# Centring the rows ahead of a feed-forward, and multiplying the normalisation's scale in at the last addition

## The chip, the cores and the metric

The kernel runs on one core of a Trainium2 chip. The metric is the device time of one execution in microseconds (us), median over runs. Profile times are in us from the first instruction of the profiled execution, or in ns where that is said. PE is the matrix engine, DVE the vector engine, ACT the scalar (activation) engine, POOL the GpSimd engine; SP issues DMAs.

## What is computed

A linear-attention layer (RWKV style) is followed by a Fourier mixing and a feed-forward with a residual. There are 4 batches of 768 rows, 8 heads of 48 columns, so a model width of 384; the feed-forward is 1536 wide.

```
for t in range(S):                       # attention, per batch and head
    cur = outer(u * k[t], v[t])
    y[t] = r[t] @ (state + cur)
    state = w[:, None] * state + outer(k[t], v[t])
x = y, heads side by side                # (4, 768, 384)
U  = x + real(fft(fft(x, axis=1), axis=2))
un = (U - mean(U)) / sqrt(var(U) + 1e-6) # per row
out = U + maximum(un @ w_ch1, 0) @ w_ch2
```

## The kernel before, in words

**Tiling.** The attention goes in 24 chunks of 128 rows, 6 to a batch. `attend(i)` (L307) does one: DVE scales keys and receptances into `KR` (L317), PE turns them (`tp`, L327), ACT copies the turned tile out (`KRT`, L330), PE makes the scores (`A_ps`, L341), which are masked into `MA` by DVE (L348) or by ACT and POOL (L353, L355); the state goes through PE (`u_ps`, L369 and L372) and DVE (`Sst`, L376); PE sums the outputs in `yd_ps` (L391, L396, L411), ACT takes its diagonal part out (`DE`, L401), POOL multiplies it by the values (`TT`, L402), and DVE adds both into `X` (L415). `fold` (L425) makes sums and differences of a batch's rows (`EO`, `XF`), `fourier(b)` (L451) does the two transforms as matrix products: the first into `mm` (L463), copied by ACT (L470), turned round by DVE (`TR`, L479); the second (`mp`, L498 to L502), to which DVE adds X in `UF` (L508). In what follows a *half* is 384 rows, half a batch: 3 blocks of 128 rows, 8 halves `hf` in all.

**Normalisation.** For each block DVE takes statistics (`st`, L513, and `MV`, L515: mean and variance). `normed` (L519) waits for all three blocks of the half: ACT takes the square root (L524), DVE the reciprocal `rstd` (L526) and `nm`, minus mean times `rstd` (L528), and ACT writes the normalised rows `UN` in bf16, one instruction for each block, with `rstd` as scale and `nm` as bias (L533). For batch 0 PE turns `UN` (L554) and DVE copies it out to `UNT` (L557); for the others one DMA transpose for each half, issued from SP (L545), does so.

**Feed-forward.** `mlp1(hf, ft)` (L573): three matrix products on `UNT` into a PSUM tile `hp` (L582), and ACT's clamp (Relu) into `HT` (L586); 12 of them make a half. `mlp2(hf, j)` (L589): twelve products on `HT` into a PSUM tile `mo` (L598), DVE adds `UF` into `osb` (L605), and POOL issues its DMA to the output (L608); 3 of them make a half.

**PSUM.** `hp`, `mo`, the tiles of both transforms, the turned rows of batch 0 and the fillers are all called "mm" and share three buffers.

**What sets the order.** The kernel is a list of operations, each with an engine, a planned duration, what it needs (`r`), what it makes (`w`), the tiles that it takes anew (`new`) and uses, and a number `pri`. `_Schedule.order` (L100) plays the list through and decides for each engine what comes next; the program is emitted in that order, and each engine then runs its instructions strictly in it. The rule of choice is L149:

```
start = max(at, o["ready"], t + self.LATENCY)
key = (start, o["pri"], o["n"])
if pick is None or key < pick[0]:
```

The operation that can start first is taken, and `pri` decides among those that can start at the same time, lowest first. `t` comes from `room(o)` (L121): a new tile of a ring of n buffers can be taken once every operation on the tile n places before it in that ring has been planned and has ended. `pri` is 10 times the chunk's number for the attention, 10 times 6(b+1), plus 5 to 7, for the transforms and the normalisation of batch b, from 10,000 up for the feed-forward's products, and -100 for the operations that take a product out of PSUM (L470, L508, L557, L586, L605, L608). `idle` (L612) puts up to 220 fillers, products of zeros, on PE at the lowest rank where nothing else can start (planned time below 46 us).

Of the kernel before, what the change touches and what calls it, by code (L numbers as in the profile page):

```python
# [9 lines left out]
AluOp = mybir.AluOpType  # L10
Act = mybir.ActivationFunctionType
AX = mybir.AxisListType
F32 = mybir.dt.float32
# [60 lines left out]
class _Schedule:  # L74
# [18 lines left out]
    def op(self, eng, ns, fn, r=(), w=(), new=(), use=(), after=(), dma=0, pri=0, until=None):  # L93
        o = dict(eng=eng, ns=ns, fn=fn, deps=list(r), after=list(after), w=list(w), new=list(new), dma=dma, pri=pri, until=until,
                 n=len(self.ops))
        for t in set(new) | set(use):
            t.ops.append(o)
        self.ops.append(o)
# [91 lines left out]
def kernel(  # L190
# [11 lines left out]
    nc = tc.nc  # L202
    cp = ctx.enter_context(tc.tile_pool(name="cp", bufs=1))
    inp = ctx.enter_context(tc.tile_pool(name="inp", bufs=6))
    wp = ctx.enter_context(tc.tile_pool(name="wp", bufs=3))
# [32 lines left out]
    eps_t = cp.tile([128, 1], F32, name="eps_t")  # L238
# [37 lines left out]
    op = sch.op  # L276
# [3 lines left out]
    def new(pool, shape, dtype, name, bufs):  # L280
        return sch.tile((pool, shape, dtype, name), name, bufs)
# [141 lines left out]
    bat = [dict() for _ in range(B)]  # L423
# [27 lines left out]
    def fourier(b):  # L451
        X, XF = bat[b]["X"], bat[b]["XF"]
        TT = new(bp, [128, 3, 2, 386], BF16, "TT2", 2)
        TR = new(bp, [128, 3, 2, 384], BF16, "TR", 1)
        pri = 10 * (NQ * b + NQ) + 5
# [30 lines left out]

        def second(sh, j, UF, MV):
            blk = sh * 3 + j
            mp = new(ps, [128, 2, 192], F32, "mm", 3)
            st = new(wp, [128, 6], F32, "st", 3)  # L490
            src = (TT, TR)[sh]
            lo = j * 128

            def mm():
                flat = mp().rearrange("p a m -> p (a m)")
                for ri in range(2):
                    tb = hid_t[:, 0 if ri == 0 else 1 + sh, :]
                    nc.tensor.matmul(flat, lhsT=src()[:, 1, ri, lo:lo + 128], rhs=tb[:, 192:576], start=(ri == 0),  # L498
                                     stop=False, skip_group_check=True)
                    nc.tensor.matmul(flat[:, 0:192], lhsT=src()[:, 0, ri, lo:lo + 128], rhs=tb[:, 0:192],  # L500
                                     start=False, stop=False, skip_group_check=True)
                    nc.tensor.matmul(flat[:, 192:384], lhsT=src()[:, 2, ri, lo:lo + 128], rhs=tb[:, 576:768],  # L502
                                     start=False, stop=(ri == 1), skip_group_check=True)

            deps = [("TR", b, c) for c in range(3)] if sh else [("TT2", b, c, p) for c in range(3) for p in range(2)]
            p2 = pri + 1 + sh
            op("PE", 660, mm, r=deps + ["hid"], w=[("mp", b, blk)], new=[mp], use=[src], pri=p2)
            op("DVE", 550, lambda: nc.vector.tensor_tensor(  # L508
                out=UF()[:, j, :].rearrange("p (m a) -> p a m", a=2), in0=mp(),
                in1=X()[:, blk, :].rearrange("p (m a) -> p a m", a=2), op=AluOp.add),  # L510
               r=[("mp", b, blk)], w=[("UF", b, blk)], new=[UF] if j == 0 else [], use=[mp, UF, X],
               after=[("UF", b, sh * 3)] if j else [], pri=-100)
            op("DVE", 550, lambda: nc.vector.bn_stats(out=st(), in_=UF()[:, j, :]), r=[("UF", b, blk)],  # L513
               w=[("st", b, blk)], new=[st], use=[UF], pri=p2)
            op("DVE", 170, lambda: nc.vector.bn_aggr(out=MV()[:, j, :], in_=st()), r=[("st", b, blk)],  # L515
               w=[("MV", b, blk)], new=[MV] if j == 0 else [], use=[MV, st],
               after=[("MV", b, sh * 3)] if j else [], pri=p2)

        def normed(sh, UF, UNT, MV):  # L519
            p2 = pri + 1 + sh  # L520
            rstd = new(wp, [128, 3], F32, "rstd", 3)
            nm = new(wp, [128, 3], F32, "nm", 3)
            UN = new(wp, [128, 3, DM], BF16, "UN", 2)
            op("ACT", 300, lambda: nc.scalar.activation(out=rstd(), in_=MV()[:, :, 1], func=Act.Sqrt, bias=eps_t[:, 0:1]),  # L524
               r=[("MV", b, sh * 3 + j) for j in range(3)], w=[("sd", b, sh)], new=[rstd], use=[MV], pri=p2)
            op("DVE", 170, lambda: nc.vector.reciprocal(out=rstd(), in_=rstd()), r=[("sd", b, sh)],  # L526
               w=[("rstd", b, sh)], use=[rstd], pri=p2)
            op("DVE", 150, lambda: nc.vector.scalar_tensor_tensor(  # L528
                out=nm(), in0=MV()[:, :, 0], scalar=-1.0, in1=rstd(), op0=AluOp.mult, op1=AluOp.mult),
               r=[("rstd", b, sh)], w=[("nm", b, sh)], new=[nm], use=[MV, rstd], pri=p2)  # L530

            def norm(j):
                op("ACT", 705, lambda: nc.scalar.activation(  # L533
                    out=UN()[:, j, :], in_=UF()[:, j, :], func=Act.Identity, scale=rstd()[:, j:j + 1],
                    bias=nm()[:, j:j + 1]), r=[("nm", b, sh), ("UF", b, sh * 3 + j)], w=[("UN", b, sh, j)],
                   new=[UN] if j == 0 else [], use=[UN, UF, rstd, nm], after=[("UN", b, sh, 0)] if j else [], pri=p2)

            for j in range(3):
                norm(j)
            if b == 0:  # L540
                for j in range(3):
                    turned(sh, j, UN, UNT)
                op("NONE", 0, lambda: None, r=[("UNT", b, sh, j) for j in range(3)], w=[("UNT", b, sh)])
                return
            op("SP", 1200, lambda: nc.sync.dma_start_transpose(  # L545
                out=UNT().rearrange("p j c t -> p (j c) t"), in_=UN().rearrange("p j d -> p (j d)")),
               r=[("UN", b, sh, j) for j in range(3)], w=[("UNT", b, sh)], new=[UNT], use=[UN], dma=1500, pri=-1000)
# [13 lines left out]
        for sh in range(2):  # L561
            UF = new(bp, [128, 3, DM], F32, "UF", 5)
            UNT = new(bp, [128, 3, 3, 128], BF16, "UNT", 5)
            MV = new(wp, [128, 3, 2], F32, "MV", 3)
            for j in range(3):
                second(sh, j, UF, MV)
            normed(sh, UF, UNT, MV)
            bat[b]["halves"].append((UF, UNT))


    HTs = {}

    def mlp1(hf, ft, pri):  # L573
        UF, UNT = bat[hf // 2]["halves"][hf % 2]
        if ft == 0:
            HTs[hf] = new(bp, [128, 12, 384], BF16, "HT", 3)
        HT = HTs[hf]
        hp = new(ps, [128, 384], F32, "mm", 3)

        def mm():  # L580
            for dt in range(3):
                nc.tensor.matmul(hp(), lhsT=W1[:, dt, ft * 128:(ft + 1) * 128], rhs=UNT()[:, :, dt, :],  # L582
                                 start=(dt == 0), stop=(dt == 2))

        op("PE", 495, mm, r=[("UNT", hf // 2, hf % 2), "W1"], w=[("hp", hf, ft)], new=[hp], use=[UNT], pri=pri)
        op("ACT", 490, lambda: nc.scalar.activation(out=HT()[:, ft, :], in_=hp(), func=Act.Relu), r=[("hp", hf, ft)],  # L586
           w=[("HT", hf, ft)], new=[HT] if ft == 0 else [], use=[hp, HT], after=[("HT", hf, 0)] if ft else [], pri=-100)

    def mlp2(hf, j, pri):  # L589
        b, sh = divmod(hf, 2)  # L590
        UF, UNT = bat[b]["halves"][sh]
        HT = HTs[hf]
        mo = new(ps, [128, DM], F32, "mm", 3)
        osb = new(wp, [128, DM], F32, "osb", 3)

        def mm(lo, hi):
            for ft in range(lo, hi):
                nc.tensor.matmul(mo(), lhsT=HT()[:, ft, j * 128:(j + 1) * 128], rhs=W2[:, ft, :],  # L598
                                 start=(ft == 0), stop=(ft == 11))

        op("PE", 985, lambda: mm(0, 6), r=[("HT", hf, ft) for ft in range(6)] + ["W2"], w=[("mo", hf, j, 0)], new=[mo],
           use=[HT], pri=pri)
        op("PE", 985, lambda: mm(6, 12), r=[("HT", hf, ft) for ft in range(6, 12)] + [("mo", hf, j, 0)],
           w=[("mo", hf, j)], use=[HT, mo], pri=pri)
        op("DVE", 555, lambda: nc.vector.tensor_tensor(out=osb(), in0=mo(), in1=UF()[:, j, :], op=AluOp.add),  # L605
           r=[("mo", hf, j)], w=[("osb", hf, j)], new=[osb], use=[mo, UF], pri=-100)
        row = (sh * 3 + j) * 128
        op("POOL", 550, lambda: nc.gpsimd.dma_start(out=out[b, row:row + 128, :], in_=osb()), r=[("osb", hf, j)],  # L608
           w=[("out", hf, j)], use=[osb], dma=500, pri=-100)
# [77 lines left out]
```

## Time and profile before

| what | value |
|---|---|
| three timed runs | 209.21, 210.62 and 217.61 us; median 210.62 |
| profiled execution, first to last instruction | 209.7 us |
| PE busy | 186.7 us (89%) |
| DVE busy | 136.0 us (65%) |
| ACT busy | 129.5 us (62%) |
| POOL busy | 64.0 us (31%) |
| last product starts its block of 48 | at 196.44 us |
| last addition `osb` starts | at 204.4 us |

The profiled execution has no time of its own beside the span; the span lies 0.5 us above the fastest timed run and 0.9 us below the median. Engines are counted busy for the union of their instructions; each engine's instructions are in the order of the program. A group's row gives the line, engine, operation, output and inputs, count, then busy time in us and the mean duration of one in ns, then the idle time of the engine just before them and what ended it. In the page's second part each digit is one fortieth of the span (5.24 us), in tenths; PEclk is the clock that PE was granted, in tenths of full speed.

### The profile page before, as it was taken

The page shows a single profiled execution, that of the slowest core. Times are in us where ns is not written, and L with a number is a line of the kernel's source. Part 1 is how long each engine was busy: PE and PEld are TensorE (multiplying, and loading weights), DVE is VectorE, ACT ScalarE, POOL GpSimd, SP SyncE. Part 2 cuts the span into 40 slices and gives each one's busy share as a digit, 9 for nine tenths or more (in the row PEclk, how much of TensorE's full clock was granted, in tenths as well). Part 3 has the DMA queues.
Part 4 walks back from the last instruction along what each step waited for, and adds up shares of the span by engine and source line. Part 5 has one row for each costly group of instructions (what it writes and reads, how often), then busy time and mean ns, then how long its engine had stood idle before and what let it go on. Part 6 is the DMA issues. An engine that isn't in the chain of part 4 may idle for free.

```text
span 209.7 us, 4438 instructions
## 1 busy us (share of the span) xinstructions
PE 186.7 (89%) x1729; PEld 118.7 (57%) x1731; DVE 136.0 (65%) x281; ACT 129.5 (62%) x260; POOL 64.0 (31%) x92
## 2 busy tenths in 40 slices
PE   7199975599999699999789999999999999999990
PEld 2056643267576366577457567666567665666550
DVE  5178999649999448899897999883739511111221
ACT  3467852562898686874678986987371895364300
POOL 5017793111038244442344323234110121121131
PEclk9969998569999999999969999999999999999999
DMA  5999999999759999967567000044110144112122
GB/s 103 181 188 190 258 219 210 182 191 172 125 106 164 193 179 219 219 131 150 113 144 150 12 3 0 30 104 94 41 38 0 42 99 126 38 41 75 38 75 75
DMA packets 86548, 24.73 MB, mean 118 GB/s; under 512 B 82944, under 2 KB 84608, under 8 KB 86528
## 3 DMA queue, kind: packets, MB, share of 16 engines
q1 hardware_dynamic: 82848, 17.37, 47.4%
q0 software_dynamic: 3680, 7.08, 13.3%
q8 instruction: 13, 0.21, 0.5%
q14 instruction: 7, 0.06, 0.1%
HBM read 20.32 MB, written 4.72 MB: 119 GB/s over the span
## 4 chain that ended last, share of the span: by engine, by line
PE 37%; issue 27%; DVE 11%; DMA 11%; POOL 6%; ACT 3%; SPq 2%; POOLq 0%; ACTq 0%; DVEq 0%
PE mm L598 7%; DMA vt<-in_v_dram 6%; PE mm L582 5%; DMA kr<-in_r_dram 5%; PE mm L614 4%; PE tp L327 4%; POOL out_dram L608 4%; PE mm L463 3%; DVE KR L317 3%; PE mm L498 3%; PE A_ps L341 2%; PE u_ps L369 2%; DVE XF L439 2%; DVE X L415 1%; PE yd_ps L411 1%
## 5 line engine op out<-in xcount | busy, mean ns | idle before, releaser
L586 ACT ACTIVATE HT<-mm 128x384 bf16<-128x384 f32 x96 | 45.9, 493 | 22.5 <-PE mm L582 22.1
L582 PE MATMUL mm<-UNT,W 128*128 128x384 bf16 x288 | 53.7, 330 | 0.5 <-DVE osb L605 0.3
L598 PE MATMUL mm<-W,HT 128*128 128x384 bf16 x288 | 51.1, 326 | 0.0
L605 DVE TENSOR_TENSOR osb<-mm,UF 128x384 f32<-128x384 f32 x24 | 13.3, 555 | 37.9 <-PE mm L598 37.9
L598 PEld LDWEIGHTS <-HT 128*128 128x128 bf16 x288 | 27.7, 98 | 17.6
L582 PEld LDWEIGHTS <-W 128*128 128x128 bf16 x288 | 27.3, 99 | 17.5 <-issue 1.4
L355 POOL TENSOR_SCALAR_AFFINE_SELECT MA<-AC 128x512 bf16<-128x512 bf16 x29 | 19.4, 676 | 50.4 <-ACT AC L353 49.3
L402 POOL TENSOR_TENSOR TT<-V,DE 128x384 bf16<-128x384 bf16 x24 | 25.0, 1040 | 27.7 <-ACT DE L401 27.0
L608 POOL DMA_DIRECT2D out_dram<-osb x24 | 13.3, 554 | 62.6 <-DVE osb L605 57.6
L317 DVE TENSOR_TENSOR KR<-kr,wtab 128x768 bf16<-128x768 f32 x24 | 24.9, 1044 | 8.6 <-ACT wtab L244 5.7
L330 ACT COPY KRT<-tp 128x1024 bf16<-128x1024 bf16 x24 | 24.5, 1019 | 6.2 <-PE tp L327 6.0
L353 ACT CAST AC<-A_ps 128x512 bf16<-128x512 f32 x29 | 16.6, 591 | 11.7 <-PE A_ps L341 11.7
L614 PE MATMUL mm<-zero 128*128 128x512 bf16 x71 | 20.1, 423 | 1.4 <-DVE wuc L233 1.3
L327 PE MATMUL tp<-ident,KR 128*128 128x128 bf16 x192 | 15.7, 229 | 5.8 <-DVE KR L317 5.6
L322 ACT CAST V<-vt 128x384 bf16<-128x384 f32 x24 | 12.0, 522 | 8.9 <-DMA vt<-in_v_dram 5.1
L327 PEld LDWEIGHTS <-KR 128*128 128x128 bf16 x192 | 12.4, 103 | 9.1 <-DVE KR L317 6.4
L533 ACT ACTIVATE UN<-UF,nm,rstd 128x384 bf16<-128x384 f32 x24 | 15.7, 699 | 2.8 <-DVE nm L528 2.8
L415 DVE TENSOR_TENSOR X<-yd_ps,TT 128x384 bf16<-128x384 f32 x24 | 13.1, 546 | 5.7 <-POOL TT L402 5.7
L470 ACT CAST TT<-mm 128x386 bf16<-128x386 f32 (+1 forms) x24 | 12.7, 600 | 4.3 <-PE mm L463 4.3
L331 DVE TENSOR_TENSOR PR<-KRT 128x512 bf16<-128x512 bf16 x24 | 14.1, 596 | 0.5 <-ACT KRT L330 0.4
L508 DVE TENSOR_TENSOR UF<-mm,X 128x384 f32<-128x384 f32 x24 | 12.7, 551 | 1.8 <-PE mm L502 1.1
L348 DVE TENSOR_TENSOR MA<-A_ps,mtri 128x512 bf16<-128x512 f32 x19 | 12.9, 681 | 1.1 <-PE A_ps L341 1.0
(67 smaller groups left out, 239.6 us busy)
## 6 DMA issues: line engine op xcount, KB each, us to landing
kr<-in_k_dram SPq DMA_DIRECT2D x24, 192.0 KB, 4.5
kr<-in_r_dram SPq DMA_DIRECT2D x24, 192.0 KB, 4.6
vt<-in_v_dram SPq DMA_DIRECT2D x24, 192.0 KB, 4.4
out_dram<-osb POOLq DMA_DIRECT2D x24, 192.0 KB, 2.2
W<-in_moe_w_ch_dram POOLq DMA_DIRECT2D x6, 384.0 KB, 7.7
hid_t<-hid_c SPq DMA_DIRECT2D x1, 576.0 KB, 5.1
te_t<-te_c SPq DMA_DIRECT2D x1, 289.5 KB, 4.3
to_t<-to_c SPq DMA_DIRECT2D x1, 288.0 KB, 4.0
```

The costliest lines, as they stand in the source:

```text
L317: op("DVE", 960, lambda: nc.vector.tensor_tensor(out=KR().rearrange("t s p (a d) -> t (s p) a d", a=2)[:, :, :, 0:D], in0=kr().rearrange(" ...
L327: nc.tensor.transpose(tp()[:, s, p, :], KR()[:, s, p, :], ident)
L330: op("ACT", 1010, lambda: nc.scalar.copy(KRT(), tp()), r=[("tp", i)], w=[("KRT", i)], new=[KRT], use=[tp], pri=pri)
L353: op("ACT", 590, lambda: nc.scalar.copy(AC(), A_ps[a]()), r=[("A", i)], w=[("AC", i, a)], new=[AC], use=[A_ps[a]], pri=pri)
L355: op("POOL", 680, lambda: nc.gpsimd.affine_select(out=MA[a](), in_=AC(), pattern=[[0, NP], [1, 128]], base=0, channel_multiplier=-1, compa ...
L402: op("POOL", 850, lambda: nc.gpsimd.tensor_tensor(out=TT(), in0=V(), in1=DE().unsqueeze(2).to_broadcast([128, H, D]), op=AluOp.mult), r=[( ...
L533: op("ACT", 705, lambda: nc.scalar.activation(out=UN()[:, j, :], in_=UF()[:, j, :], func=Act.Identity, scale=rstd()[:, j:j + 1], bias=nm() ...
L582: nc.tensor.matmul(hp(), lhsT=W1[:, dt, ft * 128:(ft + 1) * 128], rhs=UNT()[:, :, dt, :], start=(dt == 0), stop=(dt == 2))
L586: op("ACT", 490, lambda: nc.scalar.activation(out=HT()[:, ft, :], in_=hp(), func=Act.Relu), r=[("hp", hf, ft)], w=[("HT", hf, ft)], new=[H ...
L598: nc.tensor.matmul(mo(), lhsT=HT()[:, ft, j * 128:(j + 1) * 128], rhs=W2[:, ft, :], start=(ft == 0), stop=(ft == 11))
L608: op("POOL", 550, lambda: nc.gpsimd.dma_start(out=out[b, row:row + 128, :], in_=osb()), r=[("osb", hf, j)], w=[("out", hf, j)], use=[osb], ...
L614: op("PE", 216, lambda: nc.tensor.matmul(z(), lhsT=zero[:, 0:128], rhs=zero, start=True, stop=True), r=["zero"], w=[("idle", len(sch.ops)) ...
```

## The change

`UN` holds minus (row minus mean) instead of the normalised row: ACT computes it with the constant scale -1 and the mean as bias, and each block waits only for its own mean. The square root and the reciprocal stay, in the same places of the list but behind the centring, with `pri` 9000 in place of that of the batch (66 to 247), and no longer precede `UN`; `nm` is gone. The clamp multiplies by -1 before it clamps, which takes the sign back; since the scale of a row is positive it passes through the clamp and both products, and the last addition multiplies the row of `mo` by `rstd` (a scalar per partition) and adds `UF` in one instruction, `scalar_tensor_tensor` in place of `tensor_tensor`. It therefore waits for the reciprocal as well. The rings of `MV` and `rstd` grow from 3 to 8 buffers, and the buffer of `UF` is taken when the first product of the half is planned rather than when its addition is.

```
-            op("PE", 660, mm, r=deps + ["hid"], w=[("mp", b, blk)], new=[mp], use=[src], pri=p2)
+            op("PE", 660, mm, r=deps + ["hid"], w=[("mp", b, blk)], new=[mp, UF] if j == 0 else [mp], use=[src],
+               after=[("mp", b, sh * 3)] if j else [], pri=p2)
...
-        def normed(sh, UF, UNT, MV):
+        def normed(sh, UF, UNT, MV, rstd):
             p2 = pri + 1 + sh
-            rstd = new(wp, [128, 3], F32, "rstd", 3)
-            nm = new(wp, [128, 3], F32, "nm", 3)
             UN = new(wp, [128, 3, DM], BF16, "UN", 2)
+
+            def centre(j):
+                op("ACT", 705, lambda: nc.scalar.activation(
+                    out=UN()[:, j, :], in_=UF()[:, j, :], func=Act.Identity, scale=-1.0,
+                    bias=MV()[:, j, 0:1]), r=[("MV", b, sh * 3 + j), ("UF", b, sh * 3 + j)], w=[("UN", b, sh, j)],
+                   new=[UN] if j == 0 else [], use=[UN, UF, MV], after=[("UN", b, sh, 0)] if j else [], pri=p2)
+
+            for j in range(3):
+                centre(j)
             op("ACT", 300, lambda: nc.scalar.activation(out=rstd(), in_=MV()[:, :, 1], func=Act.Sqrt, bias=eps_t[:, 0:1]),
-               r=[("MV", b, sh * 3 + j) for j in range(3)], w=[("sd", b, sh)], new=[rstd], use=[MV], pri=p2)
+               r=[("MV", b, sh * 3 + j) for j in range(3)], w=[("sd", b, sh)], new=[rstd], use=[MV], pri=9000)
             op("DVE", 170, lambda: nc.vector.reciprocal(out=rstd(), in_=rstd()), r=[("sd", b, sh)],
-               w=[("rstd", b, sh)], use=[rstd], pri=p2)
-            op("DVE", 150, lambda: nc.vector.scalar_tensor_tensor(
-                out=nm(), in0=MV()[:, :, 0], scalar=-1.0, in1=rstd(), op0=AluOp.mult, op1=AluOp.mult),
-               r=[("rstd", b, sh)], w=[("nm", b, sh)], new=[nm], use=[MV, rstd], pri=p2)
-
-            def norm(j):
-                op("ACT", 705, lambda: nc.scalar.activation(
-                    out=UN()[:, j, :], in_=UF()[:, j, :], func=Act.Identity, scale=rstd()[:, j:j + 1],
-                    bias=nm()[:, j:j + 1]), r=[("nm", b, sh), ("UF", b, sh * 3 + j)], w=[("UN", b, sh, j)],
-                   new=[UN] if j == 0 else [], use=[UN, UF, rstd, nm], after=[("UN", b, sh, 0)] if j else [], pri=p2)
...
+               w=[("rstd", b, sh)], use=[rstd], pri=9000)
...
-            MV = new(wp, [128, 3, 2], F32, "MV", 3)
+            MV = new(wp, [128, 3, 2], F32, "MV", 8)
+            rstd = new(wp, [128, 3], F32, "rstd", 8)
...
-        op("ACT", 490, lambda: nc.scalar.activation(out=HT()[:, ft, :], in_=hp(), func=Act.Relu), r=[("hp", hf, ft)],
+        op("ACT", 490, lambda: nc.scalar.activation(out=HT()[:, ft, :], in_=hp(), func=Act.Relu, scale=-1.0), r=[("hp", hf, ft)],
...
-        op("DVE", 555, lambda: nc.vector.tensor_tensor(out=osb(), in0=mo(), in1=UF()[:, j, :], op=AluOp.add),
-           r=[("mo", hf, j)], w=[("osb", hf, j)], new=[osb], use=[mo, UF], pri=-100)
+        op("DVE", 555, lambda: nc.vector.scalar_tensor_tensor(
+            out=osb(), in0=mo(), scalar=rstd()[:, j:j + 1], in1=UF()[:, j, :], op0=AluOp.mult, op1=AluOp.add),
+           r=[("mo", hf, j), ("rstd", b, sh)], w=[("osb", hf, j)], new=[osb], use=[mo, UF, rstd], pri=-100)
```

More of the change, by code (lines that the diff above doesn't have):

```diff
@@ L510, in second @@
                 in1=X()[:, blk, :].rearrange("p (m a) -> p a m", a=2), op=AluOp.add),
-               r=[("mp", b, blk)], w=[("UF", b, blk)], new=[UF] if j == 0 else [], use=[mp, UF, X],
+               r=[("mp", b, blk)], w=[("UF", b, blk)], use=[mp, UF, X],
                after=[("UF", b, sh * 3)] if j else [], pri=-100)
@@ L517, in second @@
                after=[("MV", b, sh * 3)] if j else [], pri=p2)
-        def normed(sh, UF, UNT, MV):
+        def normed(sh, UF, UNT, MV, rstd):
             p2 = pri + 1 + sh
-            rstd = new(wp, [128, 3], F32, "rstd", 3)
-            nm = new(wp, [128, 3], F32, "nm", 3)
             UN = new(wp, [128, 3, DM], BF16, "UN", 2)
+            def centre(j):
[5 more added lines that the diff above has]
+                centre(j)
             op("ACT", 300, lambda: nc.scalar.activation(out=rstd(), in_=MV()[:, :, 1], func=Act.Sqrt, bias=eps_t[:, 0:1]),
-               r=[("MV", b, sh * 3 + j) for j in range(3)], w=[("sd", b, sh)], new=[rstd], use=[MV], pri=p2)
+               r=[("MV", b, sh * 3 + j) for j in range(3)], w=[("sd", b, sh)], new=[rstd], use=[MV], pri=9000)
             op("DVE", 170, lambda: nc.vector.reciprocal(out=rstd(), in_=rstd()), r=[("sd", b, sh)],
-               w=[("rstd", b, sh)], use=[rstd], pri=p2)
-            op("DVE", 150, lambda: nc.vector.scalar_tensor_tensor(
-                out=nm(), in0=MV()[:, :, 0], scalar=-1.0, in1=rstd(), op0=AluOp.mult, op1=AluOp.mult),
-               r=[("rstd", b, sh)], w=[("nm", b, sh)], new=[nm], use=[MV, rstd], pri=p2)
-            def norm(j):
-                op("ACT", 705, lambda: nc.scalar.activation(
-                    out=UN()[:, j, :], in_=UF()[:, j, :], func=Act.Identity, scale=rstd()[:, j:j + 1],
-                    bias=nm()[:, j:j + 1]), r=[("nm", b, sh), ("UF", b, sh * 3 + j)], w=[("UN", b, sh, j)],
-                   new=[UN] if j == 0 else [], use=[UN, UF, rstd, nm], after=[("UN", b, sh, 0)] if j else [], pri=p2)
-            for j in range(3):
-                norm(j)
+               w=[("rstd", b, sh)], use=[rstd], pri=9000)
             if b == 0:
@@ L563, in fourier @@
             UNT = new(bp, [128, 3, 3, 128], BF16, "UNT", 5)
-            MV = new(wp, [128, 3, 2], F32, "MV", 3)
+            MV = new(wp, [128, 3, 2], F32, "MV", 8)
+            rstd = new(wp, [128, 3], F32, "rstd", 8)
             for j in range(3):
                 second(sh, j, UF, MV)
-            normed(sh, UF, UNT, MV)
-            bat[b]["halves"].append((UF, UNT))
+            normed(sh, UF, UNT, MV, rstd)
+            bat[b]["halves"].append((UF, UNT, rstd))
     HTs = {}
     def mlp1(hf, ft, pri):
-        UF, UNT = bat[hf // 2]["halves"][hf % 2]
+        UF, UNT, _ = bat[hf // 2]["halves"][hf % 2]
         if ft == 0:
@@ L590, in mlp2 @@
         b, sh = divmod(hf, 2)
-        UF, UNT = bat[b]["halves"][sh]
+        UF, UNT, rstd = bat[b]["halves"][sh]
         HT = HTs[hf]
```

## The prediction

> **What bounds the kernel now.** I read the page's first two parts, then the table by stretches, the timelines of PE and DVE, the rows of the groups that change, and last the instruction order of the changed program (it can be built without running) against that of the old one.
>
> ```profile
> span 209.7 us, 4438 instructions
> PE 186.7 (89%) x1729; PEld 118.7 (57%) x1731; DVE 136.0 (65%) x281; ACT 129.5 (62%) x260; POOL 64.0 (31%) x92
> ...
> PE   7199975599999699999789999999999999999990
> ...
> DVE  5178999649999448899897999883739511111221
> ...
> PEclk9969998569999999999969999999999999999999
> ```
>
> PE bounds the kernel from about 51 us to the end, and DVE is nearly as full up to 145 us. The table by stretches (columns: stretch and length, busy us and count of PE, weight loads, DVE, ACT, POOL; granted clock; DMA share; GB/s) says how full:
>
> ```profile
> 15.50:28.30 12.80, 11.88 (x160) 7.82 (x160) 11.44 (x16) 10.14 (x20) 10.54 (x14) 1.00 1.21 229
> 35.00:40.00 5.00, 3.04 (x23) 1.92 (x24) 4.35 (x10) 1.19 (x2) 0.00 (x0) 0.52 0.97 186
> 51.36:107.00 55.64, 51.01 (x558) 33.80 (x557) 46.14 (x103) 42.02 (x85) 20.73 (x27) 1.00 0.86 159
> 107.00:111.00 4.00, 4.00 (x34) 2.46 (x34) 4.00 (x5) 2.26 (x6) 2.35 (x4) 0.59 0.63 123
> 107.00:145.70 38.70, 38.29 (x423) 25.68 (x423) 33.28 (x65) 31.30 (x66) 14.37 (x19) 0.96 0.28 59
> 145.70:196.44 50.74, 50.41 (x327) 31.01 (x324) 17.66 (x41) 28.71 (x60) 6.81 (x12) 1.00 0.19 56
> ```
>
> In 51 to 145 us PE alternates attention, transforms and feed-forward: what the attention leaves empty is filled with products of `mlp1` and `mlp2`. So the question is not what the edited instructions cost but whether the feed-forward still fills that stretch.
>
> ```profile
> 24.22 0.54 DVE L415 TENSOR_TENSOR X<-yd_ps,TT 128x384 bf16<-128x384 f32 x1
> ...
> 27.71 0.55 DVE L415 TENSOR_TENSOR X<-yd_ps,TT 128x384 bf16<-128x384 f32 x1
> ...
> 51.36 3.62 PE L614 MATMUL mm<-zero 128*128 128x512 bf16 x16
> 54.81 0.33 PE L554 MATMUL mm<-ident,UN 128*128 128x128 bf16 x3
> ...
> 196.44 7.96 PE L598 MATMUL mm<-W,HT 128*128 128x384 bf16 x48
> ```
>
> Read here: a chunk of attention without feed-forward takes 3.5 us; 16 fillers hold PE until the first normalised rows can be turned; the last 48 products end at 204.4, 5.3 us before the end.
>
> ```profile
> L586 ACT ACTIVATE HT<-mm 128x384 bf16<-128x384 f32 x96 | 45.9, 493 | 22.5 <-PE mm L582 22.1
> L533 ACT ACTIVATE UN<-UF,nm,rstd 128x384 bf16<-128x384 f32 x24 | 15.7, 699 | 2.8 <-DVE nm L528 2.8
> L605 DVE TENSOR_TENSOR osb<-mm,UF 128x384 f32<-128x384 f32 x24 | 13.3, 555 | 37.9 <-PE mm L598 37.9
> L528 DVE SCALAR_TENSOR_TENSOR nm<-MV,rstd 128x3 f32<-128x3 f32 x8 | 1.3, 162 | 0.3
> ```
>
> **What the Trainium skill says.** "Perfetto Trace Analysis", Optimization Strategy: a gap that repeats over a stretch on the engine that should be full can mean that there isn't enough PSUM for the next tile. The trace of before has no such stretch after 51 us. "SBUF — State Buffer", SBUF: two separate sides: DVE with two SBUF inputs and GpSimd exclude each other. The trace agrees in kind: `PR` (L331) takes 0.41 us beside an idle POOL and 0.86 to 1.05 in 16 to 28 us. "TensorE: Matmul & The Clock Gate", Part 1: a PE that was little used runs at half clock until it has been busy for some 3.4 us. The trace agrees: clock 0.52 in 35 to 40, and 0.59 for 4 us at 107, although PE was full there.
>
> **The small parts.** `nm` goes: 8 times 0.16 us on DVE, 1.3 in all. The centring keeps 24 ACT instructions; I take 0.70 us, as L533 (at least 0.52, as the plain copy of values L322, which has no pointers). The clamp with scale -1 stays at 0.49. `osb` with a scalar has no row of this size: `nm` (0.162) against the reciprocal's 0.170 shows no extra fixed cost, so I take 0.555, at most twice that. It lies beside PE, where a half's third of products takes 1.95 us; only the last one ends the kernel: 0 to +0.6, I take 0. The early square root is not needed for the rows of batch 0, so the planner puts 8 fillers where 16 were, and two behind: 13 against 19. PE reaches the first turning at 51.36 + 8 x 0.216 = 53.1 in place of 54.8: -1.7. No transfer is added: both programs issue the same DMAs. In the new order SP issues the two transposes of batch 1 ahead of four pairs of loads rather than two; in before they took 5.0 us to issue (102.3 to 107.3), so pair 21 lands at about 107, some 10 us before its use below.
>
> **What the change moves, the large part.** The square root and the reciprocal now have rank 9000. While DVE has attention work ready (ranks up to 240), a reciprocal that could start at the same time is put behind it. In the new order the reciprocal of half 0 stands behind the `KR` of chunk 14; that of half 1 stands behind the very last `KR`, of chunk 24. In between `X` of chunks 14 to 21 is made. But `mlp2` of half 1 has run two blocks by then, and their two tiles `mo` hold two of the three "mm" buffers until `osb`, which waits for this reciprocal. The planner's ring gives out buffers in order, so after one more `mlp1` (3 products) nothing of the feed-forward or of the transforms can be planned. PE's new order shows it: between the 36 products of `mlp2` and the transform of batch 2 stand 56 `tp`, 56 `A_ps`, 29 `u_ps`, 52 + 56 products for `yd_ps`, and those 3 products, nothing else. So DVE paces the stretch, and PE waits in it.
>
> When it begins: PE from 51.36 to there has 13 fillers (2.8 us), 18 turnings (1.0), 72 `mlp1` and 60 `mlp2` products at 0.1625 (21.5), the transforms of batch 1 (18 at 0.1635 and 36 at 0.109: 6.9) and attention for 7 to 8 chunks (62 `A_ps` at 0.041, 56 `tp` at 0.056, 64+28+32 for `yd_ps` at 0.026, 0.041 and 0.028, 24 `u_ps` 1.5 in all: 10.9), each by the distance of starts in the timeline: 43.0. Before left PE idle for 4.6 us in 51 to 107; I take 3.6: it begins at 98.0, and DVE's first wait on it, `Sst`, ends at 98.9.
>
> How long: from there to the last `KR` DVE has 7 `X`, 8 `MA`, 7 `Sst`, 9 `PR`, 8 `KR`, 2 `EO`, 2 `XF`: with the means of the page (0.546, 0.681, 0.550, 0.596, 1.044, 0.755, 0.887) 30.1 us, less 43 times the 0.09 by which neighbours overlap, 26.2. In 15.5 to 28.3 DVE was busy 89% with the same chain: 29.5. By the other way, 8 chunks at 3.5 and 3.3 for the fold, 31. PE has about 11 us of work in 31 and will be at a low clock for part of it; `tp` took 0.78 in place of 0.45 at 44.6. I add 2: 31.5, so the reciprocal comes at 130.4, and the first `osb` frees a buffer at 131.0.
>
> What is left: 35 and 72 products of the transforms (5.7, 7.9), 213 of `mlp1` (34.6), 228 of `mlp2` (37.1), attention 1.3: 86.6. Before ran such a stretch (145.7 to 196.4) without a gap. To this +2 for 4 us at half clock, as at 107, and +1 for the chain of the last fold. 131.0 + 86.6 + 3 + 5.3 = 225.9 against the span of 209.7. The median stands 0.9 above the span, the fastest run 0.5 below: 226.
>
> As a check: the stretch holds 33 us with 11 of work, so 22 us empty; given back are 1.3 (fillers), about 3 of PE's idle time after 98 us and 2 of its slow clock there: 209.7 + 22 - 6 = 226.
>
> **Rivals.** (a) *The stretch is quicker.* POOL has one mask less per chunk than in 15 to 28 us, so DVE may be held less: with the undisturbed distances (`KR` 0.87, `PR` 0.33, `MA` 0.60, `X` and `Sst` 0.465, fold 2.8) 24.0 us, clock kept: 122.9 + 0.6 + 86.6 + 5.3 = 215.4. For it: few masks on POOL. Against: POOL's 25.0 us of `TT` are unchanged, and each `X` waits for one. (b) *The chain of each chunk paces, not DVE.* At half clock PE needs 3.4 us a chunk, and each chunk hangs on one `tp` and one `yd_ps` buffer: 4.2 a chunk, 36.9 with the fold: 135.8 + 0.6 + 86.6 + 3 + 5.3 = 231, and 2 more for slow clock, 233. (c) *Not slower: DVE's pace.* The place is the same 43 operations. The end stays within 2% of before (under 214.8) if the reciprocal comes by 122, that is if they take 23 us, 0.54 each with all waits; without any wait they need 24.0, so this asks also for an earlier start: with no stall of PE after 51 us it would begin at 94.4, giving 212. (d) *The parts decide, the order doesn't:* -1.7 at 53 us and `nm` gone, 208. For it: that would be the sum if the order were kept. Against: the order is fixed in the program and shows the reciprocal behind the last `KR`.
>
> **Chances.** Forecast 0.70 (own range 220 to 231), (a) 0.13, (b) 0.12, (c) 0.03, (d) 0.02. A range from 216 to 234 leaves out about 2 in 10 and takes in the double price of the last `osb`. A difference of about 2% is what a measurement of this kernel can tell from none. Faster by more than that: 0.02; within 2%: 0.04; slower: 0.94.
>
> **What would show it.** Right: first turned rows on PE at about 53; PE's digits at 3 to 6 in slices from about 98 to 130 us, with PEclk below 9 in some; the second reciprocal at about 130, `osb` waiting for it with the products long done; from there PE full to the end, the output DMAs crowded behind it. Wrong: feed-forward products between 100 and 128 us; the second reciprocal before 120; or PE gaps after 135 us, which would say that the last stretch has a wait which I have missed.

## The result, and the profile after

The changed kernel takes 223.42 us in the median of four runs (222.4 to 224.74), the kernel before, beside it, 210.38: ratio 1.0615, 95% interval 1.0548 to 1.0681. It is 6% slower. Ratios leave out the slow executions that some kernels have now and then, such as before's of 217.61 us. The profiled execution spans 223.0 us, 13.3 more than before. Every timed run whose span is on record stands 1.7 us above it (224.74 and 223.0 here), so the profile of before, at 209.7, is an execution of about 211.4, 1 us above its median, and not one between the fastest and the median.

The page of the kernel after, the lines that answer to those shown of before (in the second part a slice is 5.58 us):

```profile
span 223.0 us, 4436 instructions
PE 193.2 (87%) x1723; PEld 123.9 (56%) x1725; DVE 139.2 (62%) x273; ACT 128.3 (58%) x260; POOL 64.8 (29%) x92
...
PE   7299965699999989997449599999999999999990
...
DVE  5268999559996998988997858956362212121131
...
PEclk9859997589999999999655569999999999999997
```

PE's share fell only from 89% to 87%, so the totals hide the loss. The second part shows its place: from the 19th slice (100 to 128 us) PE has the digits 7, 4, 4, 9, 5, where before has 7 and 8 up to 110 us and then 9 throughout. The one 9 in there stands over a PEclk of 5: PE at half speed looks full with half the work. That is also how 13.3 us more span splits: 6.8 us more idle PE (29.8 against 23.0), and 6.5 us more *busy* PE (193.2 against 186.7), although PE has six products fewer.

The table by stretches of the kernel after (columns as in the prediction):

```profile
51.36:107.00 55.64, 51.93 (x606) 35.03 (x604) 50.08 (x100) 43.71 (x91) 21.73 (x27) 1.00 0.89 163
98.00:131.00 33.00, 22.68 (x301) 17.23 (x299) 28.12 (x49) 17.39 (x32) 15.15 (x18) 0.65 0.40 77
131.00:218.00 87.00, 86.69 (x584) 53.57 (x582) 32.40 (x72) 47.23 (x101) 12.05 (x21) 0.99 0.19 56
```

Up to 98 us nothing is lost, and from 131 us PE has no gap to its last product (217.69). In between ACT, which clamps the feed-forward's products, is half idle too. What PE did with the shared buffers there, from the view of one tile's instructions ("mm", 98 to 133 us; columns: count, shortest, median and longest duration in ns, first and last start in us):

```profile
L463 PE MATMUL mm<-te_t,XF x8: 327/528/528, 128.9 to 132.8; 128*128 128x386 bf16 x8
L463 PE MATMUL mm<-to_t,XF x6: 326/474/527, 129.9 to 132.2; 128*128 128x384 bf16 x6
L595 PE MATMUL mm<-W,HT x5: 326/326/326, 97.7 to 98.4; 128*128 128x384 bf16 x5
L579 PE MATMUL mm<-UNT,W x3: 326/326/326, 100.2 to 100.5; 128*128 128x384 bf16 x3
...
L602 DVE SCALAR_TENSOR_TENSOR osb<-mm,rstd,UF x2: 609/614/619, 128.2 to 128.7; 128x384 f32<-128x384 f32 x2
```

The last products of `mlp2` (L595) end at 98.5, one `mlp1` (L579) goes at 100.2, then no product touches "mm" for 28 us. It is `osb` at 128.2 that frees a buffer, and 0.8 us later the transform (L463) begins. The timeline of DVE shows what `osb` waited for:

```profile
126.67 1.39 DVE L317 TENSOR_TENSOR KR<-kr,wtab 128x768 bf16<-128x768 f32 x1
127.98 0.16 DVE L534 RECIPROCAL rstd<-rstd 128x3 f32<-128x3 f32 x1
128.17 1.14 DVE L602 SCALAR_TENSOR_TENSOR osb<-mm,rstd,UF 128x384 f32<-128x384 f32 x2
```

A reciprocal of 0.16 us, whose root ACT had ready at 80.1 (L532, start 79.79), stands behind the last `KR`, and two tiles whose products were done by 98.5 wait for it.

### The profile page after: what moved, and what is told of

Its sections match the earlier page's. It is cut to its first block, busy times and chain, and to the rows that moved or that the text cites. A ratio compares the mean times of both kernels' runs of the same rounds, so it can differ in the third digit from the quotient of the medians.

```text
span 223.0 us, 4436 instructions
## 1 busy us (share of the span) xinstructions
PE 193.2 (87%) x1723; PEld 123.9 (56%) x1725; DVE 139.2 (62%) x273; ACT 128.3 (58%) x260; POOL 64.8 (29%) x92
## 4 chain that ended last, share of the span: by engine, by line
issue 37%; PE 28%; DVE 14%; DMA 6%; POOL 6%; ACT 5%; SPq 2%; POOLq 0%; ACTq 0%; DVEq 0%
DMA vt<-in_v_dram 6%; DVE KR L317 5%; PE mm L463 5%; PE tp L327 4%; POOL out_dram L606 4%; PE mm L595 3%; PE mm L579 3%; PE mm L612 3%; PE A_ps L341 2%; DVE EO L433 2%; ACT KRT L330 2%; PE mm L498 2%; DVE XF L439 2%; DVE MA L348 1%; DVE X L415 1%
## 5 line engine op out<-in xcount | busy, mean ns | idle before, releaser
L579 PE MATMUL mm<-UNT,W 128*128 128x384 bf16 x288 | 52.2, 326 | 0.0
L595 PE MATMUL mm<-W,HT 128*128 128x384 bf16 x288 | 49.9, 326 | 0.0
L602 DVE SCALAR_TENSOR_TENSOR osb<-mm,rstd,UF 128x384 f32<-128x384 f32 x24 | 14.7, 617 | 42.6 <-PE mm L595 42.4
L595 PEld LDWEIGHTS <-HT 128*128 128x128 bf16 x288 | 28.0, 98 | 18.4
L579 PEld LDWEIGHTS <-W 128*128 128x128 bf16 x288 | 27.5, 98 | 17.4 <-issue 0.2
L355 POOL TENSOR_SCALAR_AFFINE_SELECT MA<-AC 128x512 bf16<-128x512 bf16 x29 | 20.2, 703 | 42.8 <-ACT AC L353 34.6
L317 DVE TENSOR_TENSOR KR<-kr,wtab 128x768 bf16<-128x768 f32 x24 | 28.0, 1178 | 6.1 <-ACT wtab L244 5.8
L327 PE MATMUL tp<-ident,KR 128*128 128x128 bf16 x192 | 18.5, 254 | 10.1 <-DVE KR L317 9.5
L327 PEld LDWEIGHTS <-KR 128*128 128x128 bf16 x192 | 14.2, 114 | 13.7 <-DVE KR L317 11.2
L612 PE MATMUL mm<-zero 128*128 128x512 bf16 x65 | 19.6, 439 | 1.4 <-DVE wuc L233 1.3
L376 DVE TENSOR_TENSOR Sst<-u_ps,WD 128x384 bf16<-128x384 f32 x20 | 11.0, 550 | 6.0 <-PE u_ps L372 5.8
L463 PEld LDWEIGHTS <-XF 128*128 128x128 bf16 x72 | 7.5, 112 | 11.1 <-issue 6.4
```

Of the source, the lines that this page charges most:

```text
L317: op("DVE", 960, lambda: nc.vector.tensor_tensor(out=KR().rearrange("t s p (a d) -> t (s p) a d", a=2)[:, :, :, 0:D], in0=kr().rearrange(" ...
L327: nc.tensor.transpose(tp()[:, s, p, :], KR()[:, s, p, :], ident)
L355: op("POOL", 680, lambda: nc.gpsimd.affine_select(out=MA[a](), in_=AC(), pattern=[[0, NP], [1, 128]], base=0, channel_multiplier=-1, compa ...
L463: nc.tensor.matmul(fp(), lhsT=XF()[:, par, nb, cb * 128:(cb + 1) * 128], rhs=tab[:, nb, :], start=(nb == 0), stop=(nb == 2))
L612: op("PE", 216, lambda: nc.tensor.matmul(z(), lhsT=zero[:, 0:128], rhs=zero, start=True, stop=True), r=["zero"], w=[("idle", len(sch.ops)) ...
```

## The experiments

Edits are against the changed kernel unless said otherwise. Each ratio is to the kernel before, run beside it.

**Rank of root and reciprocal put back.** The new arithmetic stays whole.

```
-               r=[("MV", b, sh * 3 + j) for j in range(3)], w=[("sd", b, sh)], new=[rstd], use=[MV], pri=9000)
+               r=[("MV", b, sh * 3 + j) for j in range(3)], w=[("sd", b, sh)], new=[rstd], use=[MV], pri=p2)
...
-               w=[("rstd", b, sh)], use=[rstd], pri=9000)
+               w=[("rstd", b, sh)], use=[rstd], pri=p2)
```

> The changed kernel with one edit: the square root and the reciprocal get back the rank of their batch, all else stays (centring, sign, scale in the last addition). Theory (a reciprocal of rank 9000 comes late, so the last additions keep the mm buffers and PE stands empty): PE is filled between 98 and 130 us, 207 to 212 us. Rival 1 (centring earlier makes a worse order, whatever the rank): 218 or more. Rival 2 (the scaled last addition and the new waits cost by themselves): 213 to 217.

Measured: 205.92 us, ratio 0.98 (0.9703 to 0.9898), a little under what was expected; span 203.9. Its second part and its stretch:

```profile
PE   7189975689998999999999999999999999999990
```

```profile
98.00:131.00 33.00, 31.80 (x343) 21.42 (x342) 29.61 (x56) 25.34 (x53) 10.94 (x14) 1.00 0.44 92
```

The hole is gone: PE 31.80 of 33 us busy at full clock, where after had 22.68 at 0.65. All the loss comes from the rank 9000; the arithmetic itself costs nothing. The same kernel was timed again, beside one that has `pri=-100` in both places, ahead of all attention work:

> The changed kernel with root and reciprocal at the ranks of before, run again beside the one at rank -100, in more rounds: 204 to 208 us, ratio to before 0.97 to 0.985. If the gain of the first run of it (0.98) was chance, the ratio is 0.99 to 1.00.

> The changed kernel with root and reciprocal at rank -100, ahead of all attention work, in place of 9000. Theory (only the late reciprocal costs; once it is early enough, being earlier brings nothing): as with the ranks of before (203.9 us span), 204 to 208 us, ratio 0.97 to 0.99, feed-forward products throughout 98 to 131 us. Rival (the two small operations cut into DVE's chain, which is nearly full up to 145 us, and put ACT's table or a wait for the root in its way): 208 to 212, ratio 0.99 to 1.01.

Measured: 207.47 us, ratio 0.9885 (0.9813 to 0.9957) for the ranks of before; 208.8, 0.9936 (0.9902 to 0.9969) for -100. The gain of the early ranks over the kernel before is there both times, between 1 and 2%, though the second ratio lies between the two that were expected. Going first of all brings nothing more and seems to cost something: 208.8 and 0.9936 are what the rival expected, not the theory. ACT's table plays no part in it (two loads in either kernel, the last at about 10 us). Of the 3.3 us by which the profiled span is longer than its neighbour's (207.4 against 204.1), 1.2 lie ahead of the first rows turned (54.18 against 52.96), and from 51 to 98 us PE is busy 1.9 us less (44.28 against 46.19). Whether the two operations in DVE's chain do that is not shown.

**The wait taken out of `osb`, the rank left at 9000.** The scale of the rows is left out.

```
-            out=osb(), in0=mo(), scalar=rstd()[:, j:j + 1], in1=UF()[:, j, :], op0=AluOp.mult, op1=AluOp.add),
-           r=[("mo", hf, j), ("rstd", b, sh)], w=[("osb", hf, j)], new=[osb], use=[mo, UF, rstd], pri=-100)
+            out=osb(), in0=mo(), scalar=1.0, in1=UF()[:, j, :], op0=AluOp.mult, op1=AluOp.add),
+           r=[("mo", hf, j)], w=[("osb", hf, j)], new=[osb], use=[mo, UF], pri=-100)
```

> The changed kernel with rank 9000 kept, but the last addition multiplies by the constant 1.0 and does not wait for the reciprocal; the scale of the rows is left out, so the output is not the reference's. The reciprocals stay as late as in the changed kernel. Theory (the wait of the last addition on the late reciprocal is what holds the buffers): 207 to 212 us. Rival 1 (the earlier centring makes the worse order): 218 or more. Rival 3 (a late reciprocal or square root delays ACT or DVE directly): stays at 220 to 224.

Measured: 208.0 us, ratio 0.9895 (0.9814 to 0.9977). Of this kernel, DVE's timeline and the "mm" tile from 98 to 128 us:

```profile
124.56 0.16 DVE L534 RECIPROCAL rstd<-rstd 128x3 f32<-128x3 f32 x1
```

```profile
L579 PE MATMUL mm<-UNT,W x48: 323/326/327, 99.4 to 115.7; 128*128 128x384 bf16 x48
L595 PE MATMUL mm<-W,HT x24: 323/326/327, 98.5 to 121.1; 128*128 128x384 bf16 x24
```

The second reciprocal is as late as ever, but nobody needs it, and 72 feed-forward products run in the stretch where after had 8. A late reciprocal costs little by itself (span 206.0, against 203.9 with early ranks); what costs is that `osb` waits for it while it holds a buffer.

**Only half 1 late, and only half 1 early.** The rank of root and reciprocal, in the first kernel:

```
-  pri=9000
+  pri=9000 if (b, sh) == (0, 1) else p2
```

and in the second:

```
-  pri=9000
+  pri=p2 if (b, sh) == (0, 1) else 9000
```

> The changed kernel, rank 9000 for the square root and reciprocal of half 1 of batch 0 alone, the batch's rank for the other seven halves. Theory (one half's late reciprocal is enough, since it holds two of three mm buffers): the order again has a stretch of attention alone, and the time is 219 to 226 us. A rival in which all halves share the cost evenly: about an eighth of the 13 us, 210 to 213.

> The reverse: the batch's rank for half 1 of batch 0 alone, rank 9000 for the others. Its order has a shorter stretch of attention alone, later, in front of the reciprocals of the next halves (151 of PE's products against some 250). Theory: the same loss moves there and is smaller in proportion, 214 to 219 us. If half 1 were special for another reason than its buffers: 207 to 212. If the shares were even: 219 to 223.

Measured: half 1 late 222.34 us, 1.0581 (1.0473 to 1.069), as slow as the whole change: its reciprocal starts at 127.59, and between the `mlp2` product at 101 us and the transform at 128.58 PE's timeline has no product into "mm". Half 1 early 210.82 us, 1.001 (0.9953 to 1.0066): well under what was expected, and a number that the rival (half 1 is special for another reason than its buffers, 207 to 212) would have given. The trace tells them apart: the hole is there, ahead of half 2's late reciprocal (128.98), but it is shorter; the timeline of PE in the kernel with half 1 early, its products into "mm" alone:

```profile
117.91 0.65 PE L463 MATMUL mm<-to_t,XF 128*128 128x384 bf16 x3
...
129.19 1.14 PE L463 MATMUL mm<-te_t,XF 128*128 128x386 bf16 x3
```

From 118.5 to 129.2 PE has attention alone, 10.7 us, at full clock nearly to the end. The expectation took the loss from the kernel before; it has to be taken from the new arithmetic with early ranks: 210.0 - 203.9 = 6.1 us, of which 1.1 lies ahead of the first rows turned (54.19 against 53.13). That is 5.0, or 0.47 for each us of the hole. After lost 19.1, of which 1.2 lie ahead of that point: 17.9 for 128.9 - 98.5 less 0.5 of `mlp1`, 29.9 us, or 0.60 for each. The longer hole is dearer by the us, and it is the one in which the clock fell; that the rest is attention work which PE has to do at some time is argued, not shown.

**Which of the two late operations?** The root alone put back to `p2`, and the reciprocal alone: the first, and then the second, pair of lines of the diff above with the ranks put back.

> The changed kernel with the batch's rank for the square root on ACT alone; the reciprocal on DVE keeps 9000. Its order has a stretch of attention alone of some 119 products on PE, against 249 in the changed kernel and 151 in e4. Theory (it is the reciprocal on the full DVE that is put behind): e1 plus 0.6 us for each us of that stretch, about 8 us of stretch, 209 to 213. If ACT's square root were what comes late: 205 to 207, as e1.

> The changed kernel with the batch's rank for the reciprocal alone; the square root on ACT keeps 9000. Its order has no stretch of attention alone, since ACT has gaps to take the root in. Theory: 205 to 209 us. If the square root's rank matters as much: 212 or more.

Measured: root early 208.97 us, 0.9983 (0.9949 to 1.0016), at the lower edge of what was expected; reciprocal early 206.96, 0.9848 (0.9694 to 1.0002). Neither late operation makes the long hole of half 1 alone. The timeline of DVE with the root early:

```profile
70.63 0.23 DVE L534 RECIPROCAL rstd<-rstd 128x3 f32<-128x3 f32 x2
...
127.42 0.17 DVE L534 RECIPROCAL rstd<-rstd 128x3 f32<-128x3 f32 x1
```

Both reciprocals of batch 0 are taken at 70.6, where the program leaves DVE a free moment (in after it holds the reciprocal of half 0 at 69.67, and DVE then waits 2.4 us for POOL). With the root at `p2` half 1's root is there in time for it, at 58.4; with the root at 9000 it comes at 80.1, the moment is past, and the next one is behind the last `KR`. The other way round, with the root at 88.0 and the reciprocal at `p2`, the reciprocal gets in at 91.1, before any `osb` needs it. So the long hole wants both: a root that misses the moment, and a reciprocal that can't make its own.

The late reciprocal alone still makes a shorter hole. With the root early, half 2's root is there by 93.5, but its reciprocal comes at 127.42, and ahead of it the timeline of PE has no product into "mm" for 8.3 us, much as was expected of its order:

```profile
118.02 1.14 PE L595 MATMUL mm<-W,HT 128*128 128x384 bf16 x6
...
127.46 0.67 PE L463 MATMUL mm<-te_t,XF 128*128 128x386 bf16 x3
```

Its span is 207.3, 3.4 above early ranks, of which 0.3 lie ahead of the first rows turned (53.48): 0.37 for each us of the hole, less than with half 1 early, where it was longer. With the reciprocal early there is no hole, and of the 2.0 us of span above early ranks 1.7 lie ahead of the first rows turned (54.85): the late root alone costs next to nothing.

**A buffer of its own for `mo`.** `mo` gets one "mo" buffer, and "mm" keeps two: first with rank 9000, then with the ranks of before.

```
-        mo = new(ps, [128, DM], F32, "mm", 3)
+        mo = new(ps, [128, DM], F32, "mo", 1)
...
-        hp = new(ps, [128, 384], F32, "mm", 3)
+        hp = new(ps, [128, 384], F32, "mm", 2)
```

and so, from 3 to 2, for the tiles of both transforms, the turned rows and the fillers.

> The changed kernel with rank 9000, but the tile of the second products has a PSUM buffer of its own (one), and all else that was called mm shares two. In this order the reciprocals of the halves from 2 on still come late, behind most of the attention. Theory (the late reciprocal hurts because its waiting tiles sit in the buffers that the first products and the transforms need): within 4 us of its control e6, since only the second products wait. Rival 3 (the late reciprocal itself costs): 10 us or more above e6.

> Control for e5: the same buffers with the batch's rank for the square root and the reciprocal. With only two buffers for the first products and one for the second it may be slower than e1 (205.9) whatever the theory: 206 to 216 us.

Measured: 211.68 us, 1.0051 (1.0029 to 1.0073), and 211.15, 1.004 (1.0004 to 1.0075). With `mo` apart the rank moves 0.5 us, not 16 or 17. It is weaker evidence for the link than it looks: the new rings also gave another order, in which half 1's reciprocal was taken early (two at 69.2 us), and only half 2's was late (133.75). The run without the wait is the clean one. Two shared buffers in place of three cost the early-rank kernel 4 to 5 us (211.15 against 207.47 and 205.92), so this is no remedy.

**The price of the new last addition.** The kernel *before*, its order of instructions kept, with `osb` by `scalar_tensor_tensor` and a constant column as the scalar.

```
-        op("DVE", 555, lambda: nc.vector.tensor_tensor(out=osb(), in0=mo(), in1=UF()[:, j, :], op=AluOp.add),
+        op("DVE", 555, lambda: nc.vector.scalar_tensor_tensor(
+            out=osb(), in0=mo(), scalar=eps_t[:, 0:1], in1=UF()[:, j, :], op0=AluOp.mult, op1=AluOp.add),
```

> The kernel before with its instruction order kept, each osb made by scalar_tensor_tensor with a scalar per row (a constant column, so the feed-forward's contribution to the output is scaled away; that part of the result is changed). Theory (the new osb costs the kernel nothing but its place at the end): 24 osb at about 0.617 us in place of 0.555, 1.5 us more busy DVE in all, nearly all of it beside PE's 1.95 us per third; only the last counts, +0.06: ratio to before 0.997 to 1.003. Rival (DVE sets the pace up to 145 us, each longer osb there delays the chain): about 14 osb by 0.062 us, +0.9 us, ratio 1.004; if the form were to cost much more in place (twice 0.555), +7 us, ratio 1.03.

Measured: 211.45 us, 1.0024 (0.9979 to 1.0068), no difference that can be told; the interval takes in the rival's 1.004 as well. The group's row in this kernel and in the one without the wait, whose scalar is a constant in the instruction:

```profile
L605 DVE SCALAR_TENSOR_TENSOR osb<-mm,eps_t,UF 128x384 f32<-128x384 f32 x24 | 14.8, 615 | 36.3 <-PE mm L598 36.1
```

```profile
L602 DVE SCALAR_TENSOR_TENSOR osb<-mm,UF 128x384 f32<-128x384 f32 x24 | 13.3, 556 | 35.1 <-PE mm L595 34.9
```

## Why the prediction was right

It said 226 us, and 223.42 was measured. The mechanism was the one predicted, and the runs with the ranks put back, without the wait, and with half 1 alone late bear out its links. One link was read too simply: the prediction put the late place down to the reciprocal's rank in a full DVE. That holds for half 2, but for half 1 and its long hole the runs show that the root's rank is needed as well. And the 226 owes something to luck: it set time and span equal, while a run's time is 1.7 above its span, so that the predicted span of 225.9 meant 227.6; and the execution that was profiled, 224.74, is the slowest of the four. By its own steps:

- **First rows turned at 53.1** (-1.7). In after they start at 54.34, only 0.5 earlier than before. But PE came to the 8 fillers ahead of them at 52.60 rather than 51.36, with the same order up to there. With the ranks of before it came at 51.38, and the first turning stood at 53.13. The step is right; the executions differ by 1.2 us at this point. (Among the kernels with this order PE came to these fillers between 51.2 and 53.1, so small differences of span are partly of this kind.)
- **The stretch begins at 98.0.** On PE 98.51. On DVE the step failed in a small way: `Sst` was said to end at 98.9, on the ground that DVE waits for PE there; it ended at 97.03, with no wait.
- **43 operations take 31.5.** From 97.03 to the reciprocal at 127.98: 31.0. Among them DVE waited 2.4 us for POOL's `TT` (0.99, 0.72 and 0.72) and 1.6 for PE (0.91, 0.16, 0.51), which is the surcharge of 2 for a slow PE.
- **`osb` 0.555.** 0.617, inside the bound of twice that. The comparison with `nm` could not show it, since `nm` has its scalar in the instruction and `osb` reads it from a column. The first buffer came free at 128.8 (128.17 + 0.62) and the transform began at 128.94 rather than 131.0: the 2.1 us are in the main the early start on DVE (1.9).
- **86.6 of work, and 3.** From 128.94 to the last product's end at 217.69 are 88.75, against 89.6. The surcharges were too large: the first 12 products took 3.47 us where 1.98 is full speed (the next three took 0.50), so 1.5 for the half clock and not 2; and PE was idle 0.3 us in 131 to 218, so the chain of the last fold cost no 1. The work itself came out 0.65 longer than the sum of 86.6 and hid part of this.
- **Tail 5.3.** 223.0 - 217.69 = 5.3. The longer last `osb` cannot be seen in it.
- **`nm`, `UN`, transposes: nothing.** `UN` became quicker, 0.609 for 0.699 (said: 0.70), hidden; with early ranks the parts together cost nothing.

The miss of 2.9 us on the span is 2.1 from the start of the last stretch and 0.8 from what follows it.

The rivals. (a), a stretch at DVE's undisturbed pace (24.0), fell: DVE still waited for POOL at `X`, three times over 0.7 us, and for PE. These waits are 4.0 of the 7.0 us above 24.0; the rest are longer instructions, such as `KR` of 1.58 and 1.39 us beside 0.95. (b), a chunk's chain of 4.2 us, fell too, but not by much: from `X` at 100.41 to `X` at 129.23 are seven chunks and a fold, 28.8 us, so (28.8 - 3.3) / 7 = 3.6 a chunk. That is an average: up to 110 us a chunk took 3.0 to 3.5, and the last three, at half clock, 4.4 to 5.6, with DVE idle for 0.7 to 0.9 of each. Whether the chain paces at half clock the runs do not separate. (c) needed the reciprocal by 122; it came at 128. (d), that the parts decide, is what the kernel with early ranks does, and its 208 was too high for it: 203.9. Where its gain comes from is in part seen: 1.7 us by the fillers, and 1.3 us less idle in 98 to 131 (31.80 busy against 30.50). The rest of it was not taken apart; the one execution of before with the slow 4 us at 107, which the prediction took for a part of the order, may be some of it: with the same order and the new `osb` there was no such dip, and the span was 208.3.

What the Trainium skill says in "Perfetto Trace Analysis", Optimization Strategy, of bubbles that repeat, which can mean that there is not enough PSUM for the next tile, fits after from 100 to 128 us, with one thing added by the runs: there were buffers enough (with early ranks three fill the same stretch), and one late consumer held them.

## What to carry to other kernels

When an operand is moved from ahead of a product to behind it, ask who now waits with a PSUM buffer in hand, and give the small operations that make the operand a rank by that waiter's need, not by how far away the last use seems. In a scheduled kernel, read the new order of the engine that makes the operand before anything is priced: the 0.16 us reciprocal was cheap, and its place in DVE's queue was 6% of the kernel. Then look at the slices and the clock together, since a PE at half clock counts as busy.

## What the hardware showed that was not expected

The timeline of PE in after, at both ends of the slow clock:

```profile
101.89 0.61 PE L327 MATMUL tp<-ident,KR 128*128 128x128 bf16 x8 [0.43 <-ACT KRT L330]
...
110.31 1.03 PE L327 MATMUL tp<-ident,KR 128*128 128x128 bf16 x8 [2.11 <-DVE KR L317]
...
128.11 1.03 PE L327 MATMUL tp<-ident,KR 128*128 128x128 bf16 x8 [1.56 <-DVE KR L317]
```

The same eight products take 0.61 us, then 1.03 from 110 us on, for 20 us, though PE was idle for no more than 3.1 us at a time in there. The Trainium skill, "TensorE: Matmul & The Clock Gate", Part 1, ties the slow clock to an idle window of about 3.4 us, and the full clock to as long a busy one; here the clock fell after a gap of 2.1 us in a sparsely filled stretch. Nor does the length of a gap decide alone. In before PE came back from one of the same length at full clock, in a stretch that the prediction's table shows at 1.00:

```profile
73.17 0.24 PE L391 MATMUL yd_ps<-UW,PR 128*128 128x2 bf16 x4 [2.07 <-DVE X L415]
```

Its own slow stretch at 107 us followed gaps of 1.4 us at most, and the kernel with before's order and the new `osb` kept full clock after such a gap at the same place (1.00 from 100 to 112 us). What decides stays open. On the way back the trace agrees better: without a gap from 128.11, PE was at full speed by 132.4, 4.3 us later.

A scalar read from a column made `osb` 60 ns longer (614 to 617 ns) than one in the instruction (556), which cost as much as the plain addition (555). The scale of ACT's `UN` the other way round: with a constant in place of a column, and the column kept for the bias, 609 ns in place of 699.
